# Reordering the first loads and the first chunk's copies in a fused attention and gated-MLP kernel

## The chip, the cores and the metric

The kernel runs on one core of one Trainium2 chip. The metric is the device time of one execution in microseconds (us), as a median of several. A core has a matrix engine (TensorE, "PE" in the profile, with its weight loads as "PEld"), VectorE ("DVE"), ScalarE ("ACT"), GpSimd ("POOL") and SyncE ("SP"). SP and ACT issue the DMAs of this kernel, each on a queue of its own. The times here differ by tenths of a microsecond in 266, so two things are kept apart throughout: the time of the unprofiled rounds, and the position of single instructions in one profiled execution.

## The reference, cut to what matters

One layer normalisation feeds an attention branch (32 heads of 16, a sliding window of 256) and a bilinear gated MLP; both are added to the input.

```python
def reference(x, wqkv, wo, w_gate, w_up, w_down):     # x 1x2048x512, F = 1792
    xn = layernorm(x)
    q, k, v = split(xn @ wqkv)                        # 32 heads of 16
    p = softmax(where(causal & within 256, q k^T / 4, -1e9))
    a = (p v) @ wo
    b = ((xn @ w_gate) * (xn @ w_up)) @ w_down
    return x + a + b
```

## The kernel before: the parts that matter

The 2048 tokens are worked in 4 chunks of 4 tiles of 128 tokens. Chunk 0 has to be made before any score can be computed. For each tile x is loaded, VectorE takes statistics, ScalarE the root, VectorE the reciprocal and the scaling, TensorE transposes, and then come the projections to values, keys and queries. The kernel has a list scheduler written in Python: it walks a model of the engines, with estimated landing times, and emits each instruction where the model starts it. So the order on each engine is fixed when the program is built, and the constants in the model decide it. Two of them are penalties in us: 0.3 makes ScalarE less attractive for an operation that VectorE can take too, and HOLD puts off operations that are not on the chain to the next transpose, until the first scores are placed. At the start and behind tile 0's transpose TensorE runs filler matmuls of ones.

```python
# loads, in order of issue (two queues)
load(nc.sync,   Wqkv[:, 0:2, 1024:1536], ...)   # half of Wv on SP
load(nc.scalar, x[:, 0, :], ...)                # x0 on ACT
load(nc.sync,   Wqkv[:, 2:4, 1024:1536], ...)   # other half of Wv on SP
load(nc.scalar, x[:, 1, :], ...)                # x1 on ACT
for t, lo in ((2, 512), (3, 0)):                # Wk, x2, Wq, x3 on SP
    load(nc.sync, Wqkv[:, :, lo:lo + 512], ...)
    load(nc.sync, x[:, t, :], ...)
... # Wg, Wu, rest of x, Wd in four pieces, Wo
# which engine takes an operation: the least of
key = (at + (0.3 if e == "A" and len(o.on) > 1 else 0.0) + (HOLD if o.rank and now0 else 0.0), o.rank, t)
...
# chunk 0 as the model sees it (us)
land = (3.4, 3.95, 7.7, 9.6)      # x0 to x3
wv, wk, wq = 5.9, 7.3, 9.3
# tile 1's statistics are taken in two halves; the first may run before tile 0 is scaled
...
def project(i, lo, tok=tok):      # keys or queries of one tile, into one PSUM bank
    for c in range(4):
        matmuls(M[i][:, 128*c:128*c+128], [(Wqkv[:, k, lo+128*c:...], xnT[0][:, k, tok]) for k in range(4)])
```

The softmax here doesn't subtract the row's maximum and nothing guards it: scores larger than these inputs give would overflow.

Of the kernel before, what the change touches and what calls it, by code (L numbers as in the profile page):

```python
# [18 lines left out]
SWITCH = 0.11  # L19
PE_LAT = {"V": 0.22, "A": 0.31}  # L20
LAT = 0.06
PSUM_COPY = {"V": (0.605, 0.69), "A": (0.49, 0.60)}


# [61 lines left out]
class Kernel:  # L86
# [2 lines left out]
    PACE = 2.9  # L89
    SHARE = 1.0  # L90
    FEED = 0.1
    HOLD = 0.1

    def __init__(self, live=True):
        self.live = live
# [47 lines left out]
    def prologue(self):  # L143
        nc = self.nc
        xv = self.x_d.rearrange("(t p) d -> p t d", p=128)
        w = {k: v.rearrange("(k p) n -> p k n", p=128) for k, v in self.w_d.items()}

        def load(eng, dst, src):
            eng.dma_start(out=dst, in_=src)  # L149

        load(nc.sync, self.Wqkv[:, 0:2, 1024:1536], w["qkv"][:, 0:2, 1024:1536])
        load(nc.scalar, self.x[:, 0, :], xv[:, 0, :])
        load(nc.sync, self.Wqkv[:, 2:4, 1024:1536], w["qkv"][:, 2:4, 1024:1536])
        load(nc.scalar, self.x[:, 1, :], xv[:, 1, :])
        for t, lo in ((2, 512), (3, 0)):
            load(nc.sync, self.Wqkv[:, :, lo:lo + 512], w["qkv"][:, :, lo:lo + 512])
            load(nc.sync, self.x[:, t, :], xv[:, t, :])
        h = self.F // 2
        for lo in (0, h):
            load(nc.sync, self.Wg[:, :, lo:lo + h], w["g"][:, :, lo:lo + h])  # L160
            load(nc.sync, self.Wu[:, :, lo:lo + h], w["u"][:, :, lo:lo + h])
            if lo == 0:
                load(nc.sync, self.x[:, 4:8, :], xv[:, 4:8, :])
        load(nc.sync, self.x[:, 8:NT, :], xv[:, 8:NT, :])
        for f, g in ((0, 4), (4, 8), (8, 11), (11, 14)):
            load(nc.sync, self.Wd[:, f:g], w["d"][:, f:g])
        load(nc.sync, self.Wo[:], w["o"])
        for _ in range(4):
            nc.sync.drain()

        c = self.const
        nc.gpsimd.memset(self.ident[:], 0.0)
        nc.gpsimd.affine_select(out=self.ident[:], in_=self.ident[:], compare_op=ALU.not_equal, fill=1.0,
                                base=0, pattern=[[-1, 128]], channel_multiplier=1)
        nc.gpsimd.memset(self.mhalf[:], -0.5)
        warm = c.tile([128, 1], F32, name="warm")
        nc.vector.memset(warm[:], 0.0)
        nc.vector.memset(self.eps[:], 1e-5)
        nc.scalar.activation(out=warm[:], in_=warm[:], func=ACT.Sqrt)
        self.warm = warm  # L180
        pi = c.tile([128, 1], I32, name="pi")
        nc.gpsimd.iota(pi[:], pattern=[[0, 1]], base=0, channel_multiplier=1)
        podd = c.tile([128, 1], I32, name="podd")
        nc.vector.tensor_scalar(out=podd[:], in0=pi[:], scalar1=4, scalar2=1,
                                op0=ALU.arith_shift_right, op1=ALU.bitwise_and)
        nc.vector.tensor_copy(out=self.own[:, 1:2], in_=podd[:])
        nc.vector.tensor_scalar(out=self.own[:, 0:1], in0=podd[:], scalar1=0, scalar2=None, op0=ALU.is_equal)
        nc.gpsimd.memset(self.V[0][:, :, :, 16:18], 1.0)
        self.keep_busy(42, 0)
# [98 lines left out]
    def run(self):  # L288
        if self.live:
            self.prologue()  # L290
        self.now, self.mode = 5.4, "D"
        self.free = {"V": 3.0, "A": 4.5, "G": 3.0, "S": 6.0}
        self.waiting, self.log, self.idle = [], [], []
        self.banks = [0.0] * 4
        self.s_free, self.p_free = 0.0, [0.0] * self.PBUFS
        self.at_ = {}
        self.A, self.B = [], []
        self.g = self.v = 0
        self.first_s = None
        self.credit = 0.0  # L300
        self.pairs = [(T, c) for T in range(NCH) for c in range(4)]
        self.batches, self.of_pair = [], []
        for T, c in self.pairs:
            batches = layout(T)
            self.of_pair.append(range(len(self.batches), len(self.batches) + len(batches)))
            self.batches += [(T, c, b) for b in batches]
        self.list_work()
        self.loop()
        return max(self.now, *self.free.values(), *(o for o in self.at_.values() if isinstance(o, float)))
# [20 lines left out]
    def loop(self):  # L330
        while True:
            best, now0 = None, self.first_s is None
            for o in self.waiting:
                t = self.when(o.deps)
                if t is None:
                    continue
                for e, (took, lat) in o.on.items():
                    at = max(t, self.free[e])
                    key = (at + (0.3 if e == "A" and len(o.on) > 1 else 0.0) + (self.HOLD if o.rank and now0 else 0.0), o.rank, t)
                    if best is None or key < best[0]:  # L340
                        best = (key, o, e, at)
            p = self.choose()
            if p is not None and (best is None or p[0] <= best[3]):
                self.do(*p)
                continue
            if best is None:
                break
            _, o, e, at = best
            took, lat = o.on[e]
            o.start, o.eng, o.end = at, e, at + lat + LAT  # L350
            self.free[e] = at + took
            self.waiting.remove(o)
            self.log.append((at, e, took, o.name))
            if self.live:
                o.emit(e)
            for f in o.then:
                f(o)
        left = [o.name for o in self.waiting] + [d.name for d in self.A] + [d.name for d in self.B]
        assert not left and self.g == len(self.batches) and self.v == len(self.pairs), left[:9]
# [215 lines left out]

    def first_chunk(self):

        land = (3.4, 3.95, 7.7, 9.6)
        wv, wk, wq = 5.9, 7.3, 9.3
        nc = self.nc  # L580
        roots = []
        for b in range(4):
# [26 lines left out]
                self.at_["ap", b, n] = self.op(f"ap{b}", {"V": took}, [s], lambda e, b=b, cols=cols: self.i_apply(b, cols), rank=0)  # L609
        self.op("table", {"A": (1.5, 1.5)}, roots + [("Q", 0, 0, 2)], lambda e: nc.scalar.activation(  # L610
            out=self.warm[:], in_=self.warm[:], func=ACT.Exp), rank=1)
        last = self.op("masks", {"V": (0.15, 0.2)}, [self.at_["ap", 1, 0]], lambda e: nc.vector.memset(self.masks[:], -1), rank=9)
        for n in range(5):
            last = self.op("masks", {"G": (0.4, 0.5)}, [last], lambda e, n=n: self.i_masks(n), rank=9)
        self.at_["masks",] = last
# [3 lines left out]
        for b in range(4):  # L619
            tok = slice(128 * b, 128 * b + 128)  # L620
# [13 lines left out]
                x.then.append(lambda o: self.at_.update({("begun", 0, b, ks.start): o.start}))  # L634

            def project(i, lo, tok=tok):
                for c in range(4):
                    self.matmuls(self.M[i][:, 128 * c:128 * c + 128],
                                 [(self.Wqkv[:, k, lo + 128 * c:lo + 128 * c + 128], self.xnT[0][:, k, tok]) for k in range(4)])

            def k_out(o, i, b=b):
                x = o
                for lane in range(2):
                    x = self.op(f"K0b{b}", PSUM_COPY, [o, x], lambda e, lane=lane: self.i_keys(
                        e, 0, slice(0, 4), lane, self.M[i].rearrange("p (c t) -> p c t", c=4), slice(2 * b, 2 * b + 2)), rank=1)
                self.frees(x, i)
                for c in range(4):
                    self.at_["K", 0, c, b] = x
# [53 lines left out]
    def add_qk(self, T, c):  # L702
        def emit(i, lo):
            self.matmuls(self.M[i][:], [(self.Wqkv[:, k, lo:lo + 128], self.xnT[T % 2][:, k, :]) for k in range(4)])

        def k_out(o, i):
            x = o
            for lane in range(2):
                x = self.op(f"K{T}.{c}", PSUM_COPY, [o, x], lambda e, lane=lane: self.i_keys(
                    e, T, slice(c, c + 1), lane, self.M[i].unsqueeze(1)), rank=1)  # L710
            self.frees(x, i)
            for b in range(4):
                self.at_["K", T, c, b] = x

        def q_out(o, i):
            x = self.op(f"Q{T}.{c}", PSUM_COPY, [o], lambda e: self.copy(e, self.Q[T % 2][:, c, :], self.M[i][:]), rank=1)
            self.frees(x, i)
            for b in range(4):
                self.at_["Q", T, c, b] = x

        old = self.ring(T, 2) if T == 3 else []
        self.add(f"k{T}.{c}", 4, self.xT(T) + old, lambda i: emit(i, 512 + 128 * c), k_out)
        self.add(f"q{T}.{c}", 4, self.xT(T) + self.ring(T, 2), lambda i: emit(i, 128 * c), q_out)
# [109 lines left out]
```

## Time and profile before

| | before |
|---|---|
| time, median of the first 3 runs | 265.79 us (265.54 to 265.85) |
| profiled span | 264.0 us |
| TensorE busy | 259.4 us (98%) |
| first transpose, third transpose, first scores on TensorE | 5.53, 10.58, 17.33 us |
| start of TensorE's last matmul, and from it to the end of the span | 260.22, 3.76 us |

TensorE is the bound: from the first transpose on it holds work with no pause over 0.3 us. Read such a profile by asking where its queue has holes, and then which chain feeds the work that stands behind the hole. The lines are in the prediction.

### The profile page before, as it was taken

How to read it: one execution, taken by the hardware profiler on the slowest of the kernel's cores; microseconds unless marked ns; L12 is line 12 of the kernel's file. 1: busy time of each engine (PE TensorE's matmuls, PEld its weight loads, DVE VectorE, ACT ScalarE, POOL GpSimd, SP SyncE). 2: the span in 40 equal slices, each digit the busy share in tenths (PEclk: the TensorE clock that was granted, in tenths of full speed). 3: DMA queues.
4: the chain of work that ended last, by engine and by line, in shares of the span. 5: the costliest groups of instructions: out<-in, count | busy, mean ns of one | idle time of the engine just before them, and what ended most of it. 6: DMA issues, size and time to landing. Idle time of an engine off the chain costs nothing.

```text
span 264.0 us, 8009 instructions
## 1 busy us (share of the span) xinstructions
PE 259.4 (98%) x3456; PEld 131.9 (50%) x3456; DVE 190.6 (72%) x368; ACT 165.0 (63%) x122; POOL 119.7 (45%) x272
## 2 busy tenths in 40 slices
PE   8999999999999999999999999999999999999994
PEld 7974444554444354455534354546535353545462
DVE  4999886978996548777997467786946268786504
ACT  3457576768776766687776767677777676572000
POOL 1406655475175635427084736437081828255000
PEclk9999999999999999999999999999999999999999
DMA  6999910000002200000005200000000100000002
GB/s 219 381 374 350 215 22 1 2 0 2 4 2 59 64 22 22 0 2 2 2 0 83 62 22 0 4 2 0 2 2 22 40 4 22 2 0 2 0 2 81
DMA packets 17251, 13.88 MB, mean 53 GB/s; under 512 B 7104, under 2 KB 17216, under 8 KB 17216
## 3 DMA queue, kind: packets, MB, share of 16 engines
q1 hardware_dynamic: 16784, 13.05, 18.0%
q8 instruction: 27, 0.44, 0.7%
q10 hardware_dynamic: 432, 0.33, 0.4%
q14 instruction: 8, 0.07, 0.1%
HBM read 9.70 MB, written 2.10 MB: 45 GB/s over the span
## 4 chain that ended last, share of the span: by engine, by line
PE 96%; DMA 2%; DVE 1%; ACTq 0%; issue 0%
PE M L207 72%; PE S L215 9%; PE M L245 7%; PE M L689 6%; DMA x<-in_A_x_dram 1%; DMA out_dram<-xn 1%; PE M L624 1%; PE S L207 1%; DVE xn L783 1%; DVE st L591 0%; ACTq L149 0%; DVE xn L273 0%; PE M L197 0%; DVE rs L603 0%
## 5 line engine op out<-in xcount | busy, mean ns | idle before, releaser
L498 ACT ACTIVATE P<-S 128x2048 bf16<-128x2048 f32 x76 | 140.9, 1854 | 57.1 <-PE S L215 50.5
L224 POOL TENSOR_SCALAR_AFFINE_SELECT P<-P 64x256 bf16<-64x256 bf16 (+1 forms) x248 | 112.6, 456 | 112.9 <-ACT P L498 100.7
L207 PE MATMUL M<-xnT,Wg 128*128 128x512 bf16 x224 | 57.7, 380 | 0.0
L207 PE MATMUL M<-xnT,Wu 128*128 128x512 bf16 x224 | 57.7, 380 | 0.0
L207 PE MATMUL M<-Wd,hT 128*128 128x512 bf16 (+1 forms) x224 | 51.8, 373 | 0.0
L741 DVE TENSOR_TENSOR hT<-M,gsb 128x512 bf16<-128x512 f32 x56 | 38.0, 678 | 8.4 <-PE M L207 8.1
L207 PEld LDWEIGHTS <-hT 128*128 128x128 bf16 x238 | 21.7, 98 | 23.4 <-issue 2.1
L207 PEld LDWEIGHTS <-Wu 128*128 128x128 bf16 x224 | 20.5, 98 | 24.8 <-issue 1.8
L207 PEld LDWEIGHTS <-Wg 128*128 128x128 bf16 x224 | 20.2, 98 | 24.3 <-issue 2.4
L203 DVE CAST gsb<-M 128x512 bf16<-128x512 f32 x41 | 28.1, 686 | 5.3 <-PE M L207 4.9
L207 PE MATMUL M<-xnT,Wqkv 128*128 128x128 bf16 (+1 forms) x224 | 30.3, 288 | 0.0
L215 PE MATMUL S<-Q,K 32*128 32x320 bf16 (+3 forms) x720 | 30.0, 254 | 0.0
L534 DVE STREAM_TRANSPOSE at<-M 128x512 f32<-128x512 f32 x32 | 21.3, 698 | 9.7 <-PE M L245 9.6
L215 PEld LDWEIGHTS <-K 32*128 32x128 bf16 x720 | 11.9, 92 | 31.8 <-issue 30.9
L230 DVE TENSOR_TENSOR P<-P,masks 128x512 int16<-128x512 int16 x56 | 22.6, 410 | 7.1 <-ACT P L498 7.1
L207 PEld LDWEIGHTS <-Wqkv 128*128 128x128 bf16 x224 | 15.9, 98 | 10.6 <-issue 1.5
L783 DVE TENSOR_TENSOR y<-M,x 128x512 bf16<-128x512 f32 x12 | 8.2, 687 | 16.5 <-PE M L207 16.3
L245 PE MATMUL M<-P,V 64*17 64x320 bf16 (+4 forms) x1440 | 19.5, 252 | 0.0
L245 PEld LDWEIGHTS <-V 64*17 64x17 bf16 x1440 | 17.1, 86 | 3.2 <-issue 1.3
L284 DVE TENSOR_SCALAR K<-M,own 128x512 bf16<-128x512 f32 x24 | 17.1, 743 | 2.1 <-PE M L207 2.1
L207 PE MATMUL M<-Wo,OT 128*128 128x512 bf16 (+1 forms) x64 | 16.6, 374 | 0.0
L689 PE MATMUL M<-Wqkv,xnT 128*64 128x256 bf16 x256 | 15.5, 274 | 0.0
(51 smaller groups left out, 138.0 us busy)
## 6 DMA issues: line engine op xcount, KB each, us to landing
Wg<-in_B_w_gate_dram SPq DMA_DIRECT2D x2, 896.0 KB, 10.2
Wu<-in_B_w_up_dram SPq DMA_DIRECT2D x2, 896.0 KB, 11.9
out_dram<-y SPq DMA_DIRECT2D x12, 128.0 KB, 1.7
Wqkv<-in_A_wqkv_dram SPq DMA_DIRECT2D x2, 512.0 KB, 6.1
x<-in_A_x_dram SPq DMA_DIRECT2D x1, 1024.0 KB, 13.6
Wd<-in_B_w_down_dram SPq DMA_DIRECT2D x2, 512.0 KB, 11.6
Wd<-in_B_w_down_dram SPq DMA_DIRECT2D x2, 384.0 KB, 8.7
Wqkv<-in_A_wqkv_dram SPq DMA_DIRECT2D x2, 256.0 KB, 3.5
```

Source lines behind the costliest of these rows:

```text
L203: self.nc.vector.tensor_copy(out=out, in_=in_)
L207: self.nc.tensor.matmul(ps, lhsT=a, rhs=b, start=first and n == 0, stop=last and n == len(pairs) - 1)
L215: self.nc.tensor.matmul(self.S[:, e, 64 * at:64 * (at + m)], lhsT=self.K[U % 3][rows, c, j].rearrange("p l t -> p (l t)"), rhs=self.Q[T % ...
L224: self.nc.gpsimd.affine_select(out=v, in_=v, pattern=[[0, 4], [0, n], [sign, 64]], base=0, fill=0.0, compare_op=ALU.is_gt if kind else ALU ...
L230: self.nc.vector.tensor_tensor(out=v, in0=v, in1=m, op=ALU.bitwise_and)
L245: self.nc.tensor.matmul(banks[lane][32 * e:32 * e + 17, 64 * q:64 * (q + m)], lhsT=self.V[U % 3][rows, j, 4 * c + e, 0:17], rhs=P[rows, e, ...
L284: self.nc.vector.tensor_scalar(out=out, in0=in_, scalar1=own, scalar2=None, op0=ALU.mult)
L498: ex = self.op(f"exp{g}", {"A": (took + 0.06, took + 0.18)}, [o], lambda e: self.nc.scalar.activation(out=P[:, :, 0:hi], in_=self.S[:, :, ...
L534: t = self.op(f"tr{v}", {"V": (0.63, 0.71)}, [o] + ts, lambda e, par=par: nc.vector.transpose(out=self.at[:, :, par, :], in_=self.M[banks[ ...
L689: self.nc.tensor.matmul(self.M[i][64 * lane:64 * lane + 64, 256 * jj:256 * jj + 256], lhsT=self.xnT[T % 2][:, k, tok], rhs=w[:, lane], sta ...
L741: x = self.op(f"u{T}.{f}", {"V": PSUM_COPY["V"]}, [o, ("gate", T, f)], lambda e: self.nc.vector.tensor_tensor(out=self.hT[T % 2][:, f, :], ...
L783: self.nc.vector.tensor_tensor(out=keep["y"][:, cols], in0=self.M[i][:, cols], in1=self.x[:, t, cols], op=ALU.add)
```

## The change

The intent is to have tile 1 and the second half of Wv arrive in balance on two queues, to let key projections begin when half of their weights are there, and to spread chunk 0's copies evenly over VectorE and ScalarE. The core of the diff (Wd in three pieces in place of four, new estimates for the key copies, earlier start times of the model for TensorE and ScalarE, and the mask memset after tile 3 in place of tile 1 are left out):

```diff
-        load(nc.sync, self.Wqkv[:, 2:4, 1024:1536], ...)
-        load(nc.scalar, self.x[:, 1, :], xv[:, 1, :])
-        for t, lo in ((2, 512), (3, 0)): ...
+        load(nc.sync, self.x[:, 1, :], xv[:, 1, :])
+        load(nc.scalar, self.Wqkv[:, 2:4, 1024:1536], ...)
+        load(nc.sync, self.Wqkv[:, 0:2, 512:1024], ...)      # key weights, two k halves
+        load(nc.sync, self.Wqkv[:, 2:4, 512:1024], ...)
 ...
-    HOLD = 0.1
+    HOLD = 0.2
-  key = (at + (0.3 if e == "A" and len(o.on) > 1 else 0.0) + ...
+  key = (at + (0.3 if e == "A" and len(o.on) > 1 and not now0 else 0.0) + ...
-        land = (3.4, 3.95, 7.7, 9.6);   wv, wk, wq = 5.9, 7.3, 9.3
+        land = (3.4, 4.0, 8.0, 9.85);   wv, wk, wq = 5.2, 7.1, 9.5
-                for c in range(4):
-                    self.matmuls(self.M[i][:, 128 * c:...], [... for k in range(4)])
+                for k in range(4):
+                    for c in range(4):
+                        self.nc.tensor.matmul(self.M[i][:, 128 * c:...], ..., start=k + c == 0, stop=k == 3)
```

More of the change, by code (lines that the diff above doesn't have):

```diff
@@ L21 @@
 LAT = 0.06
+KEYS_COPY = {"V": (0.68, 0.76), "A": (0.63, 0.70)}
 PSUM_COPY = {"V": (0.605, 0.69), "A": (0.49, 0.60)}
@@ L152, in prologue @@
         load(nc.scalar, self.x[:, 0, :], xv[:, 0, :])
-        load(nc.sync, self.Wqkv[:, 2:4, 1024:1536], w["qkv"][:, 2:4, 1024:1536])
-        load(nc.scalar, self.x[:, 1, :], xv[:, 1, :])
-        for t, lo in ((2, 512), (3, 0)):
-            load(nc.sync, self.Wqkv[:, :, lo:lo + 512], w["qkv"][:, :, lo:lo + 512])
-            load(nc.sync, self.x[:, t, :], xv[:, t, :])
+        load(nc.sync, self.x[:, 1, :], xv[:, 1, :])
+        load(nc.scalar, self.Wqkv[:, 2:4, 1024:1536], w["qkv"][:, 2:4, 1024:1536])
+        load(nc.sync, self.Wqkv[:, 0:2, 512:1024], w["qkv"][:, 0:2, 512:1024])
+        load(nc.sync, self.Wqkv[:, 2:4, 512:1024], w["qkv"][:, 2:4, 512:1024])
+        load(nc.sync, self.x[:, 2, :], xv[:, 2, :])
+        load(nc.sync, self.Wqkv[:, :, 0:512], w["qkv"][:, :, 0:512])
+        load(nc.sync, self.x[:, 3, :], xv[:, 3, :])
         h = self.F // 2
@@ L164, in prologue @@
         load(nc.sync, self.x[:, 8:NT, :], xv[:, 8:NT, :])
-        for f, g in ((0, 4), (4, 8), (8, 11), (11, 14)):
+        for f, g in ((0, 5), (5, 10), (10, 14)):
             load(nc.sync, self.Wd[:, f:g], w["d"][:, f:g])
@@ L290, in run @@
             self.prologue()
-        self.now, self.mode = 5.4, "D"
-        self.free = {"V": 3.0, "A": 4.5, "G": 3.0, "S": 6.0}
+        self.now, self.mode = 4.8, "D"
+        self.free = {"V": 3.0, "A": 3.4, "G": 3.0, "S": 6.0}
         self.waiting, self.log, self.idle = [], [], []
@@ L338, in loop @@
                     at = max(t, self.free[e])
-                    key = (at + (0.3 if e == "A" and len(o.on) > 1 else 0.0) + (self.HOLD if o.rank and now0 else 0.0), o.rank, t)
+                    key = (at + (0.3 if e == "A" and len(o.on) > 1 and not now0 else 0.0) + (self.HOLD if o.rank and now0 else 0.0), o.rank, t)
                     if best is None or key < best[0]:
@@ L576, in first_chunk @@
     def first_chunk(self):
-        land = (3.4, 3.95, 7.7, 9.6)
-        wv, wk, wq = 5.9, 7.3, 9.3
+        land = (3.4, 4.0, 8.0, 9.85)
+        wv, wk, wq = 5.2, 7.1, 9.5
         nc = self.nc
@@ L611, in first_chunk @@
             out=self.warm[:], in_=self.warm[:], func=ACT.Exp), rank=1)
-        last = self.op("masks", {"V": (0.15, 0.2)}, [self.at_["ap", 1, 0]], lambda e: nc.vector.memset(self.masks[:], -1), rank=9)
+        last = self.op("masks", {"V": (0.15, 0.2)}, [self.at_["ap", 3, 0]], lambda e: nc.vector.memset(self.masks[:], -1), rank=9)
         for n in range(5):
@@ L636, in project @@
             def project(i, lo, tok=tok):
-                for c in range(4):
-                    self.matmuls(self.M[i][:, 128 * c:128 * c + 128],
-                                 [(self.Wqkv[:, k, lo + 128 * c:lo + 128 * c + 128], self.xnT[0][:, k, tok]) for k in range(4)])
+                for k in range(4):
+                    for c in range(4):
+                        self.nc.tensor.matmul(
+                            self.M[i][:, 128 * c:128 * c + 128], lhsT=self.Wqkv[:, k, lo + 128 * c:lo + 128 * c + 128],
+                            rhs=self.xnT[0][:, k, tok], start=k + c == 0, stop=k == 3, skip_group_check=True)
             def k_out(o, i, b=b):
@@ L643, in k_out @@
                 for lane in range(2):
-                    x = self.op(f"K0b{b}", PSUM_COPY, [o, x], lambda e, lane=lane: self.i_keys(
+                    x = self.op(f"K0b{b}", KEYS_COPY, [o, x], lambda e, lane=lane: self.i_keys(
                         e, 0, slice(0, 4), lane, self.M[i].rearrange("p (c t) -> p c t", c=4), slice(2 * b, 2 * b + 2)), rank=1)
@@ L708, in k_out @@
             for lane in range(2):
-                x = self.op(f"K{T}.{c}", PSUM_COPY, [o, x], lambda e, lane=lane: self.i_keys(
+                x = self.op(f"K{T}.{c}", KEYS_COPY, [o, x], lambda e, lane=lane: self.i_keys(
                     e, T, slice(c, c + 1), lane, self.M[i].unsqueeze(1)), rank=1)
```

## The prediction

> **What bounds the kernel now.** I read the page first, for the busy shares. Then the view of who waited for whom, TensorE alone; then the timeline from 0 to 18 us, where every changed instruction but the later key copies lies; then the landing times of the first DMAs.
>
> The page:
>
> ```profile
> PE 259.4 (98%) x3456; PEld 131.9 (50%) x3456; DVE 190.6 (72%) x368; ACT 165.0 (63%) x122; POOL 119.7 (45%) x272
> PE 96%; DMA 2%; DVE 1%; ACTq 0%; issue 0%
> ```
>
> TensorE is busy 259.4 of 264.0 us, and the chain that ends last runs over it for 96%. Busy is not yet working, so I asked for its waits; this is the whole answer:
>
> ```profile
> PE M L197 <- PEq L817: 0.8, 1, 0.8
> PE M L624 <- DVE xn L273: 0.2, 1, 0.2
> ```
>
> Two waits in 264 us: 0.8 us of start-up and 0.2 us before the first transpose (line 624). The last copies and stores after TensorE's end make up the rest, and the change leaves them alone. So the kernel is one TensorE queue from 5.53 us on, and time can be won only where that queue holds less than it shows. I therefore compared the start-to-start distances of single matmuls, which the views merge, with the distance in the middle of a run: 56 ns for a 128-column matmul, 216 ns for a 512-column one, 109 ns for a lane pair of value projections. From 17.3 us to the end nothing exceeds these but the step from one kind of block to another (312 in place of 216 ns at the end of a dense block, about 0.1 us each). All real slack is before 10.6 us:
>
> ```profile
> 5.53 0.54 PE L624 MATMUL M<-ident,xn 128*128 128x128 bf16 x4 [0.22 <-DVE xn L273]
> 5.91 0.39 PE L197 MATMUL M<-const-bfloat16-1.0 128*128 128x128 bf16 x4
> 6.29 1.06 PE L689 MATMUL M<-Wqkv,xnT 128*64 128x256 bf16 x16
> 7.40 0.40 PE L624 MATMUL M<-ident,xn 128*128 128x128 bf16 x4
> 7.63 2.92 PE L207 MATMUL M<-xnT,Wqkv 128*128 128x128 bf16 x48
> 10.58 0.40 PE L624 MATMUL M<-ident,xn 128*128 128x128 bf16 x4
> 10.81 1.95 PE L207 MATMUL M<-xnT,Wqkv 128*128 128x128 bf16 x32
> ```
>
> The columns are start, duration, instruction, count. The reader is to see: the 48 projections need 48 x 0.056 = 2.68 us, but 2.95 us pass until the next transpose. In the single starts, 0.08 us is lost after the first 16 and 0.19 us at the end, waiting for tile 2's transpose. The same count gives 0.21 us before tile 1's transpose at 7.40, and 0.15 + 0.38 us around the split first transpose, fillers included. With the 0.22 us wait that is 0.22 + 0.53 + 0.21 + 0.08 + 0.19 = 1.23 us of slack, **0.5% of the time**: all that a change to the prologue can reach. From 10.58 to 17.3 us the queue has no holes.
>
> Why the first transpose is late (VectorE, ScalarE):
>
> ```profile
> 4.14 0.18 DVE L593 BATCH_NORM_AGGREGATE mv<-st 128x2 f32<-128x6 f32 x1
> 4.35 0.29 ACT L600 ACTIVATE ve<-mv,eps 128x1 f32<-128x1 f32 x1 [1.12 <-DVE mv L593]
> 4.60 0.43 DVE L591 BATCH_NORM_STATS2 st<-x 128x6 f32<-128x256 bf16 x1 [0.29 <-DMA x<-in_A_x_dram]
> 4.95 0.15 DVE L603 RECIPROCAL rs<-ve 128x1 f32<-128x1 f32 x1
> ```
>
> The root was ready at 4.64 us, but its reciprocal stands behind tile 1's first half of statistics, which waited until 4.58 us for x1 to land. That holds the chain by 4.95 - 4.70 = about 0.25 us.
>
> **What the Trainium skill says.** "TensorE: Matmul & The Clock Gate", Architectural detail, says ScalarE and VectorE are strict FIFO: the trace agrees (the reciprocal at 4.95 with its input ready at 4.64). The same page, Back-to-back issue gap, gives N/2.4 + 2.5 ns, so 56 ns at 128 columns, but about 81 ns for sustained pairs of load and matmul; this trace has 56 ns with a fresh weight load each, so no pair cost is there for the new loop order to save. "DMA: Bandwidth & Descriptors", Issuing engines are not separate DMA queues, says queues of SP and ACT share the same 16 engines and interleave: the packets of both queues do overlap here from 2.4 to 4.3 us. "PSUM — Partial Sum Buffer", The four PSUM rules, says a first-matmul flag clears a whole bank's bits, so one flag per bank serves k by k; no run shows that yet.
>
> **The change part by part.**
>
> *Loads.* The same bytes are moved; only order and queue differ. x1 landed at 1.25 + 3.33 = 4.58 us; by the packets, ACT's queue finished x0 near 3.0 and x1 near 4.2, SP's the first half of Wv at 3.6 and the second at 4.57 us. Starved stretches (SP's queue moves only 6 to 12 KB per 0.1 us at 3.6 to 3.8 us, against 37 later) look like issues served one after another: x0, Wv, x1, Wv. Now x1 is second on SP, so its packets begin near 3.6 us and share the engines with the 256 KB on ACT: 128 KB at half of 37 KB per 0.1 us is 0.7 us, done at 4.3; landings came 0.4 us after, so 4.7 us, or 5.0 if it goes strictly last. My choice is 4.75: **+0.15 us** at the first transpose. At best x1 lands before 4.3, and the gain stops at 0.25, as the fillers end near 5.3 us. Wv needed by 6.29 landed at 5.1; either way it is in time. Key weights landed near 7.5, and key projections start at 7.63: not a wait now, but it would be one if everything moved 0.2 us earlier. The two halves remove that, worth nothing by themselves. Bytes ahead of x2, Wq and x3 are the same, so about 7.9, 9.35 and 9.7 us stay; the new constants in the source suggest 0.2 later.
>
> *k by k.* 128 matmuls at 56 ns either way: **0**.
>
> *Copies alike.* In the loop, ScalarE loses a penalty of 0.3 in chunk 0. By walking the rule by hand I get the same TensorE order (first transpose, values 0, transpose 1, keys 0 and 1, queries 0, transpose 2), but tile 1's transposed copy goes to ScalarE, where it takes 0.60 in place of 0.41 us on VectorE but starts near 7.87, not 8.14. So keys 1 need not wait: **-0.08 us**. VectorE loses that copy, and the mask memset (0.33 us, at 7.35) moves behind tile 3. Its value copy then starts near 7.42, not 7.59, and tile 2's statistics near 8.1 in place of 8.46. The walk still puts one key copy (0.72 us) ahead of tile 2's reciprocal, so its normalised tile comes near 10.3, not 10.52: **-0.19 us** at most. Queries 0 would start at 9.42 and may wait for Wq at about 9.4 to 9.55: +0.05 to 0.1 of it back.
>
> *Later.* Key copies of later chunks are only estimated longer; no instruction changes, and nothing there waits. But the greedy order will shift, and each block more or less costs about 0.1 us: 0 +- 0.2. Three Wd loads for four: hidden, 0.
>
> Sum: +0.15 - 0.08 - 0.19 + 0.07 = **-0.05 us**, spread about 0.35.
>
> **Rivals.** (a) x1 lands earlier than now. For: someone put it ahead of the second half of Wv on SP and set the model's start to 4.8. Against: the sharing above. It would add -0.25 and give near 265.2. (b) x1 goes strictly last and lands at 5.0: first transpose +0.4, half of it absorbed, about 266.0. (c) VectorE or ScalarE becomes the bound before the first scores: VectorE is busy 6.57 of 6.70 us from 10.6 to 17.3, ScalarE 4.05. For a loss: a root behind a 0.63 us key copy on ScalarE delays a transpose. For a gain: ScalarE takes work. TensorE has gate and up blocks to fill in, so either is worth little. (d) The larger hope, scores starting earlier and everything with them: not supported, as the score pace only places blocks in a full queue, and 16 us of dense work (243.9 to 260.2 us) follows the last attention block.
>
> **Range and chances.** The sum says 265.7; as (a) is what the edit aims at and an edit of a tuned kernel is rarely made to lose, I lean to **265.55 us**. The slack of 1.23 us caps a gain near 264.6; a loss over 0.7 needs two bad terms. Eight in ten: 264.9 to 266.2. 2% is 5.3 us, over four times the slack: within 2% 0.98, each side 0.01.
>
> **What would show it.** x1's landing (4.58 now), the reciprocal (4.95), the first transpose (5.53), the third (10.58), the end of the last query projection (15.50): I expect about 4.75, 5.1, 5.7, 10.5, 15.4. TensorE's waits stay at two, and the prologue's difference plus 0.1 us per block more or fewer should be the whole difference. Wrong if TensorE shows a new wait after 17.3 us, if the 128 projections leave 56 ns, or if a block order with several more switches costs over 0.5 us.

## The result, and the profile after

The changed kernel took **266.41 us** (median of 6 runs, 266.16 to 266.46) against 265.75 us for the kernel before. The ratio is 1.0021 (95% interval 1.0008 to 1.0034): the mean time of one kernel's fast runs over that of the other's of the same rounds, so not quite the ratio of the medians. That is about 0.6 us slower, clear of noise, far within 2%, and outside the range stated. All runs count as fast: none was more than 1.5% above the fastest of its kernel.

The page of the changed kernel has less busy time on TensorE in a longer span, so the difference is waiting:

```profile
span 264.5 us, 7999 instructions
PE 259.0 (98%) x3456; PEld 131.4 (50%) x3456; DVE 189.0 (71%) x364; ACT 167.0 (63%) x126; POOL 119.7 (45%) x272
```

TensorE's waits are again two, but the 0.2 us before the first transpose (line 624 before, 627 now) has become 1.4 us (columns: us in total, times, longest):

```profile
PE M L627 <- DVE xn L276: 1.4, 1, 1.4
PE M L200 <- PEq L822: 0.8, 1, 0.8
```

The timeline of TensorE in the changed kernel (start, duration, instruction, count; fillers and the lines from 13.64 to 18.14 left out), to be laid beside the one in the prediction:

```profile
6.32 0.54 PE L627 MATMUL M<-ident,xn 128*128 128x128 bf16 x4 [1.39 <-DVE xn L276]
7.08 1.06 PE L694 MATMUL M<-Wqkv,xnT 128*64 128x256 bf16 x16
8.18 0.40 PE L627 MATMUL M<-ident,xn 128*128 128x128 bf16 x4
8.42 2.84 PE L642 MATMUL M<-xnT,Wqkv 128*128 128x128 bf16 x48
11.10 0.39 PE L627 MATMUL M<-ident,xn 128*128 128x128 bf16 x4
11.32 1.06 PE L642 MATMUL M<-xnT,Wqkv 128*128 128x128 bf16 x16
12.53 1.05 PE L642 MATMUL M<-xnT,Wqkv 128*128 128x128 bf16 x16
13.42 0.39 PE L627 MATMUL M<-ident,xn 128*128 128x128 bf16 x4
18.14 0.40 PE L218 MATMUL S<-Q,K 32*128 32x256 bf16 x8
```

The first transpose is at 6.32 in place of 5.53 us. (That is 0.79 us, while the wait grew by 1.17: the fillers before it ended 0.39 us earlier in this execution.) The 48 projections from 8.42 now need 2.68 us until the next transpose, where they needed 2.95. After queries 1 (from 11.32) there is a new hole: the next 16 projections (keys 2) start at 12.53, where 16 x 0.056 after 11.32 would be 12.22.

VectorE in the changed kernel shows why the first transpose is late:

```profile
4.23 0.18 DVE L596 BATCH_NORM_AGGREGATE mv<-st 128x2 f32<-128x6 f32 x1
5.39 0.43 DVE L594 BATCH_NORM_STATS2 st<-x 128x6 f32<-128x256 bf16 x1 [0.97 <-DMA x<-in_A_x_dram]
5.73 0.15 DVE L606 RECIPROCAL rs<-ve 128x1 f32<-128x1 f32 x1
```

The order is the one of before: tile 1's first half of statistics stands ahead of tile 0's reciprocal. But it waited for x1 until 5.37 us, where it waited until 4.58 before. Here is the account of the two profiled spans, each step read from where TensorE stands (from starts rounded to 0.01 us):

| from | before | after | difference |
|---|---|---|---|
| to the first transpose | 5.53 | 6.32 | +0.79 |
| to the third transpose | 5.05 | 4.78 | -0.27 |
| to the fourth transpose | 2.02 | 2.32 | +0.30 |
| to the first scores | 4.73 | 4.72 | -0.01 |
| to TensorE's last matmul | 242.89 | 243.00 | +0.11 |
| to the end of the span | 3.76 | 3.34 | -0.42 |
| sum | 263.98 | 264.48 | +0.50 |

Two theories could explain this. Theory 1: x1's later landing is the cause; it reaches TensorE by the order on VectorE, and the new copies give and take about the same (0.27 us before the third transpose, 0.30 after it). Theory 2: the new sharing of copies and the block order cost the time, and the late tile would have been absorbed by the holes behind it.

### The profile page after: what moved, and what is told of

It reads as the page before. It is cut to its first block, busy times and chain, and to the rows that moved or that the text cites. A ratio compares the mean times of both kernels' runs of the same rounds, so it can differ in the third digit from the quotient of the medians.

```text
span 264.5 us, 7999 instructions
## 1 busy us (share of the span) xinstructions
PE 259.0 (98%) x3456; PEld 131.4 (50%) x3456; DVE 189.0 (71%) x364; ACT 167.0 (63%) x126; POOL 119.7 (45%) x272
## 4 chain that ended last, share of the span: by engine, by line
PE 94%; DMA 2%; DVE 2%; ACT 0%; issue 0%; SPq 0%
PE M L210 69%; PE S L218 9%; PE M L248 7%; PE M L694 6%; DMA x<-in_A_x_dram 2%; PE M L642 1%; DVE st L594 1%; DMA out_dram<-xn 1%; PE S L210 1%; DVE xn L788 1%; DVE xn L276 0%; PE M L627 0%; DVE V L206 0%; DVE K L287 0%; ACT xnT L204 0%
## 5 line engine op out<-in xcount | busy, mean ns | idle before, releaser
L206 DVE CAST gsb<-M 128x512 bf16<-128x512 f32 x40 | 27.4, 686 | 6.4 <-PE M L210 6.1
L210 PE MATMUL M<-xnT,Wqkv 128*128 128x512 bf16 x96 | 23.0, 380 | 0.0
L287 DVE TENSOR_SCALAR K<-M,own 128x512 bf16<-128x512 f32 x22 | 15.7, 742 | 2.6 <-PE M L210 1.9
L204 ACT ACTIVATE gsb<-M 128x512 bf16<-128x512 f32 x16 | 9.6, 599 | 8.0 <-PE M L210 7.9
```

Of the source, the lines that this page charges most:

```text
L206: self.nc.vector.tensor_copy(out=out, in_=in_)
L210: self.nc.tensor.matmul(ps, lhsT=a, rhs=b, start=first and n == 0, stop=last and n == len(pairs) - 1)
L287: self.nc.vector.tensor_scalar(out=out, in0=in_, scalar1=own, scalar2=None, op0=ALU.mult)
```

## The experiments

All kernels but the two repeats differ from one of the two by a few lines, all gave correct results, and each was timed in 5 rounds beside the kernel before on the same chip (its median there was 265.54 to 265.71 us).

**The change with the old queues.** Only the queues of x1 and the second half of Wv go back.

```diff
 # on the changed kernel
-        load(nc.sync, x[:, 1, :]);  load(nc.scalar, Wqkv[:, 2:4, 1024:1536])
+        load(nc.sync, Wqkv[:, 2:4, 1024:1536]);  load(nc.scalar, x[:, 1, :])
```

> The changed kernel with one thing undone: x1 behind x0 on ACT and both halves of Wv on SP again. Theory 1 (x1's landing is the cause): x1 lands near 4.6 us in place of 5.37, the first transpose starts near 5.5 us in place of 6.32, and the time falls by 0.6 to 0.9 us to about 265.6, a little under or at the kernel before. Theory 2 (the new sharing of copies between ScalarE and VectorE and the block order cost the time, and the late tile is absorbed): stays above 266.1.

Measured: 265.38 us (265.31 to 266.02), ratio to before 0.9993 (0.9981 to 1.0005). x1 landed at 4.31 us, and these are the first transpose and the first scores:

```profile
5.27 0.64 PE L627 MATMUL M<-ident,xn 128*128 128x128 bf16 x4
17.24 0.40 PE L218 MATMUL S<-Q,K 32*128 32x256 bf16 x8
```

Undoing this one exchange takes back the whole loss.

**The exchange alone.** The same two lines exchanged in the kernel before, nothing else.

```diff
 # on the kernel before
-        load(nc.sync, Wqkv[:, 2:4, 1024:1536]);  load(nc.scalar, x[:, 1, :])
+        load(nc.sync, x[:, 1, :]);  load(nc.scalar, Wqkv[:, 2:4, 1024:1536])
```

> The kernel before with the one exchange: x1 on SP behind half of Wv, the other half on ACT behind x0. Theory 1: x1 lands near 5.3, the first transpose near 6.3, and the time rises by 0.7 to 0.8 us to about 266.5. Theory 2: the later holes close up (tile 2's transpose waited 0.19 us, tile 1's 0.21) and the time stays under 266.0.

Measured: 266.39 us, ratio 1.0032 (1.0020 to 1.0044). x1 landed at 5.37 us, as in the changed kernel, and the first scores came 0.79 us later than in the kernel before, as the first transpose did. Its wait for a tile, its VectorE timeline and its first scores:

```profile
PE M L624 <- DVE xn L273: 0.8, 1, 0.8
5.39 0.43 DVE L591 BATCH_NORM_STATS2 st<-x 128x6 f32<-128x256 bf16 x1 [1.05 <-DMA x<-in_A_x_dram]
5.74 0.15 DVE L603 RECIPROCAL rs<-ve 128x1 f32<-128x1 f32 x1
18.11 0.40 PE L215 MATMUL S<-Q,K 32*128 32x256 bf16 x8
```

Theory 1 stands, theory 2 falls: the holes behind did not close up at all (5.04 us from the first to the third transpose, 5.05 before). The landing view of the same stretch, for the kernel before and for this one (KB, us from issue to landing), puts it in two lines: the same 128 KB took 3.3 us on ACT behind x0, and 4.0 us on SP behind half of Wv. In all profiles taken, x1 landed at 5.28 to 5.37 us in the three with the new queues, and at 4.28 to 4.76 in eleven of the twelve with the old ones (the twelfth comes below).

```profile
x<-in_A_x_dram ACTq DMA_DIRECT2D x1, 128.0 KB, 3.3
```
```profile
x<-in_A_x_dram SPq DMA_DIRECT2D x1, 128.0 KB, 4.0
```

**Both tiles first.** Is SP slow, or is it what stands ahead of x1?

```diff
 # on the changed kernel: x1 stays on SP, but first
-        SP: half of Wv, x1, ...     ACT: x0, half of Wv
+        SP: x1, half of Wv, ...     ACT: x0, half of Wv
```

> The changed kernel with x1 still on SP and half of Wv still on ACT, but x1 ahead of SP's half of Wv. If x1 was late for what stood before it in SP's queue and shared the engines with it (my theory), x1 lands by 4.4 us and the time is near 265.4, like the old queues. If x1 was late because SP's queue as such is slow to start, it lands after 4.8 and the time stays above 266.

Measured: 265.51 us. x1 landed at 3.50 us, on SP. So it is not the queue, but what stands ahead of x1 and what shares the engines with it (256 KB and the other half of Wv in the change); the run does not part these two. But x0 landed at 3.67 us, later than the 3.3 to 3.5 of most other profiles, and the first transpose came at 5.57, no earlier than in the kernel before.

**The true landing told to the scheduler.** The loads of the change untouched; the estimate for x1 goes from 4.0 to 5.4 us, and with it tile 1's statistics go behind tile 0's reciprocal and scaling (later copies and projections shift as well).

```diff
 # on the changed kernel
-        land = (3.4, 4.0, 8.0, 9.85)
+        land = (3.4, 5.4, 8.0, 9.85)
```

> The changed kernel, loads untouched, with the scheduler told when x1 really lands (5.4 in place of 4.0), so that tile 0's reciprocal and scaling stand ahead of tile 1's statistics on VectorE. If x1 reached TensorE only through the queue order on VectorE, the first transpose is back near 5.4 us although x1 still lands near 5.4, and the time is near 265.7. If the late x1 costs whatever the order (tile 1 itself is needed), the first scores still start near 18.1 and the time stays near 266.3.

Measured: 265.70 us, with x1 landing at 5.28. Its VectorE and TensorE:

```profile
4.41 0.18 DVE L596 BATCH_NORM_AGGREGATE mv<-st 128x2 f32<-128x6 f32 x1
4.95 0.16 DVE L606 RECIPROCAL rs<-ve 128x1 f32<-128x1 f32 x1 [0.36 <-ACT ve L603]
5.15 0.60 DVE L276 TENSOR_SCALAR xn<-x,mv,rs 128x256 bf16<-128x256 bf16 x2
```
```profile
5.55 0.54 PE L627 MATMUL M<-ident,xn 128*128 128x128 bf16 x4 [0.86 <-DVE xn L276]
9.12 1.05 PE L642 MATMUL M<-xnT,Wqkv 128*128 128x128 bf16 x16 [0.52 <-DVE xnT L206]
17.64 0.40 PE L218 MATMUL S<-Q,K 32*128 32x256 bf16 x8
```

The reciprocal no longer waits for a tile that it does not need, and the first transpose is back at 5.55 us although x1 is as late as in the changed kernel. So the late landing did its harm through the order on VectorE. Of the first scores' delay 0.40 us remains (17.64 against 17.24 with the old queues). 0.28 of it is there at the first transpose: x0 landed at 3.65 us in this execution, at 3.30 in the other. The late tile itself now shows as a wait of 0.52 us before keys 1 (at 9.12), but the new order has no hole before keys 2, so that from the first transpose to the first scores it is 12.08 against 11.97 us.

**The new copies alone.** The kernel before with the changed scheduling, but its own loads and loop order.

```diff
 # on the kernel before: ScalarE's penalty off in chunk 0, HOLD 0.2, new landing and copy estimates,
 # start times of the model, mask memset after tile 3; nothing else
```

> The kernel before with the changed scheduling alone (ScalarE without its penalty in chunk 0, the new constants, the mask memset after tile 3), loads and loop order as before. Theory 1: the first transpose stays near 5.5, the third comes at 10.3 in place of 10.58, a hole of about 0.3 us before keys 2 gives it back, and the time is within 0.2 us of 265.75. Theory 2: 266.2 or more.

Measured: 265.80 us, ratio 1.0006 (0.9993 to 1.0019). The third transpose came at 10.34 us, though mostly because x1 landed at 4.28 us here and the first transpose came at 5.27. From the second to the third transpose it took 2.91 us in place of 3.18, as in the changed kernel, and the hole before keys 2 was 0.43 us. The copies give and take, as theory 1 has it. The end of this run is that of the changed kernel too: 3.30 us behind TensorE's last matmul, in place of 3.76.

**The loop and the key halves.**

```diff
 # on the kernel before: for k, for c in place of for c, for k; and the key weights in two loads
```

> The kernel before with key weights in two halves and chunk 0's projections k by k, nothing else. Theory 1: 56 ns a matmul as before, no difference over 0.15 us. Rival: interleaved sums in one bank cost time, then the 128 projections take more than 56 ns each and the time rises by more than 0.3 us.

Measured: 266.36 us, ratio 1.0029 (1.0017 to 1.0041). Neither expectation held: 0.6 us slower, with 56 ns a matmul as before. The next two runs split it.

> Half of the previous run that came out 0.6 us slower against every expectation: the kernel before with the k by k loop alone. Theory A (the loop order costs): near 266.3. Theory B (the key weights' two loads cost): near 265.7. Theory C (neither; a build has an offset of its own in when its first load lands and its last store is taken): near 265.7 too, but then the other half is no slower either.

The loop alone: 265.63 us, ratio 1.0005 (0.9992 to 1.0017). Nothing, as predicted.

> The other half: the kernel before with the key weights loaded in two k halves, old loop. Theory A: near 265.7. Theory B: near 266.3, with x1 or x0 landing later or the last store later than in the kernel before. Theory C: near 265.7.

The key halves alone: 266.44 us, ratio 1.0032 (1.0018 to 1.0045). Its first scores came at 17.36 us and TensorE's last matmul at 260.26, as in the kernel before. The loss is all behind that: 4.44 us to the end in place of 3.76. Here is the end in the kernel before and in this one (the SP line merges the last two stores, start and duration of both together):

```profile
260.38 0.81 SPq L790 DMA_DIRECT2D out_dram<-xn  x2
261.06 0.35 ACTq L790 DMA_DIRECT2D out_dram<-xn  x1
```
```profile
260.41 1.17 SPq L792 DMA_DIRECT2D out_dram<-xn  x2
261.09 0.35 ACTq L792 DMA_DIRECT2D out_dram<-xn  x1
```

SP issued the last of its stores 0.43 us later (at 261.25 against 260.82 us), though VectorE's result was there as before, and that store landed 2.14 us after its issue where it took 1.60. ACT's last store was issued as before, and it too landed late, 2.11 us after its issue in place of 1.63. The change itself does not show this. It has one load more for the keys and one less for Wd. The next two runs take that up.

```diff
 # on the kernel with the key halves; then, second, on the kernel before
-        for f, g in ((0, 4), (4, 8), (8, 11), (11, 14)):      # Wd in four loads
+        for f, g in ((0, 5), (5, 10), (10, 14)):              # in three
```

> The kernel before with the key weights in two loads and Wd in three in place of four, so SP issues as many DMAs as before. The key halves alone cost 0.7 us, all of it after TensorE's end (last store issued 0.43 us later, the end's waits 0.4 us longer). If that comes from one more DMA in SP's stream, this run is back at 265.65 and its last store follows within 0.5 us of TensorE's last matmul; if it comes from the key weights' smaller loads themselves, it stays near 266.4.

Measured: 265.57 us (265.36 to 265.63), and the end is as in the kernel before, 3.73 us behind TensorE's last matmul:

```profile
260.14 0.81 SPq L792 DMA_DIRECT2D out_dram<-xn  x2
260.82 0.35 ACTq L792 DMA_DIRECT2D out_dram<-xn  x1
```

So one DMA more on SP cost 0.7 us at the far end of the kernel. The change has as many as before, as it loads Wd in three pieces; the changed kernel with four was not run.

> The kernel before with Wd in three loads in place of four: one DMA less on SP. If only one more than before hurts (SP's stream then reaches a point it does not reach with fewer), this is 265.65 or a little less. If any change of the count hurts (the eight completion flags turn by one), it is near 266.3.

One DMA less: inconclusive, with a median of 266.03 us and a ratio of 1.0016 (1.0001 to 1.0031). Three of the six runs were at 265.64 to 265.85 us, three at 266.21 to 266.81, all at the full clock. The profile, of a run of 265.64, shows the ordinary end of 3.76 us. What the slower three had is not seen. What SP does in the gap of 0.43 us with one DMA more is open too. This profile shows something else: its first key projections waited 0.27 us (until 7.82) for the key weights, one load that landed at 7.78 us. That is the wait that the two halves are to remove; in the changed kernel the second half was there at 6.68.

**Tile 2's copy.** The hole before keys 2 stood behind ScalarE in the changed kernel:

```profile
10.36 1.27 ACT L285 ACTIVATE K<-M,own 128x512 bf16<-128x512 f32 x2 [0.34 <-DVE K L287]
11.70 0.29 ACT L603 ACTIVATE ve<-mv,eps 128x1 f32<-128x1 f32 x1
11.90 0.58 ACT L204 ACTIVATE xnT<-M 128x512 bf16<-128x512 bf16 x1
```

The transpose of tile 2 was on TensorE at 11.10 us, but its copy ran on ScalarE behind two key copies and tile 3's root. In the kernel before it ran on VectorE, and there was no hole:

```profile
11.26 0.39 DVE L203 COPY xnT<-M 128x512 bf16<-128x512 bf16 x1
```

The first try exchanges that copy with queries 0's copy:

```diff
 # on the changed kernel with the old queues
-        took = {"A": (0.48, 0.6), "V": (0.31, 0.41)} if len(ks) == 4 else ...
+        took = {"V": (0.31, 0.41)} if b == 2 else ...          # and HOLD 0.3
```

> The changed kernel with the old queues of x1 and Wv, and with tile 2's transposed copy and queries 0's copy exchanged between ScalarE and VectorE (nothing else in the two engines' order moves in chunk 0). If sharing the copies alike is what makes the 0.31 us hole before keys 2, the hole goes, and the time falls by 0.3 us against the run with the old queues alone, to about 265.1. If the hole comes from elsewhere (bank, weights), it stays and so does the time, 265.4.

Measured: 265.87 us, a miss for both sides. The scheduler answered by putting transpose 3 ahead of keys 2, where it waited 0.48 us for tile 3. Its profiled run also had x1 landing at 5.36 us with the old queues, and took 266.61 us; the other four took 265.62 to 266.02. So once in twelve profiles the old queues landed x1 as late as the new ones, and that run lost as much. The second try holds TensorE's order with one more dependence (transpose 3 after keys 2):

> The old queues in the changed kernel, tile 2's transposed copy on VectorE, and now TensorE's order held (transpose 3 after keys 2), which the earlier attempt did not hold. If the 0.31 us hole before keys 2 is tile 2's copy standing behind two key copies on ScalarE, keys 2 follow queries 1 without a hole and the first scores come 0.2 to 0.3 us earlier than with the old queues alone (17.24), with a time near 265.1. If the hole only moves to transpose 3, the time is 265.4 or more.

Measured: 265.52 us. The hole was gone, but the first scores came at 17.25 us as with the hole, because this execution began later: x1 landed at 4.54 us, the first transpose came at 5.49 in place of 5.27, and the second 2.12 us after it in place of 2.00 (the record of TensorE's full clock begins at 6.8 us here, at 5.9 there). So the pair was run again on one chip:

> The changed kernel with the old queues once more, unchanged, as the partner of the next run on the same chip: 265.4, with the hole of 0.3 us before keys 2.

> The closed hole once more, unchanged, on the same chip as the old queues. If the hole is a real part of the time: 0.3 us under its partner, 265.1. If start-up and the later waits absorb it: equal within 0.15 us.

Measured: 265.44 us with the hole, 265.29 without. The trace without it:

```profile
10.27 0.39 PE L627 MATMUL M<-ident,xn 128*128 128x128 bf16 x4
10.49 1.95 PE L642 MATMUL M<-xnT,Wqkv 128*128 128x128 bf16 x32
12.28 0.39 PE L627 MATMUL M<-ident,xn 128*128 128x128 bf16 x4
```

The 32 projections run through (10.49 to 12.28 us is 32 x 0.056), where the partner lost 0.31 us in the middle. From the third transpose to the first scores it is 6.74 against 7.05 us. In the time the medians differ by 0.15 us; one run of 267.20 us widens the interval (0.9977 to 1.0021 against before), and without it the means differ by 0.25. That is what the hole is worth by the trace, but these rounds alone do not prove it.

**A version ahead of both.** Both tiles first, and the closed hole.

> The closed hole of the previous run with x0 first on ACT and x1 first on SP, the halves of Wv behind them. If both gains add and x0 does not land later for it: 265.2, and ahead of the kernel before by 0.4. If x0 lands later beside x1 (3.67 in place of 3.3 to 3.5 in the run with both first), what is won behind is lost in front: 265.5.

Measured: **265.17 us** (264.98 to 265.36), ratio to before 0.9985 (0.9973 to 0.9997). The gain of 0.4 us is small, but its interval lies below 1. x0 landed at 3.65 us and the first transpose came at 5.55, so the front was not better than before. In the profile 0.15 us of the gain lie between there and the scores (11.65 in place of 11.79 us) and 0.47 at the end (3.28 in place of 3.76). So the exchange of the first loads does not earn it: beside the closed hole with the old queues (265.29, or 265.23 as a mean without the run of 267.20 us) it is the same within noise.

The ends of all profiled runs fall into three groups. With the old schedule it is 3.71 to 3.76 us from TensorE's last matmul to the end of the span, with one DMA more on SP 4.44 and 4.59, and with the new schedule 3.25 to 3.35. In the old schedule VectorE's last drain starts about 0.4 us after SP's and ACT's (263.47 against 263.08 us in the kernel before); in the new one it starts right beside them (264.06 against 264.03 in the changed one). VectorE has 364 instructions there in place of 368 (363 in one). That the new schedule makes the shorter end is shown by the run with the new copies alone. By what means is open. The traces have one hint: the transfers of 8 KB on the DMA queue that the profile lists as "q14 instruction", counted from 12 us before the span to just after it, are 17 in the two runs with one DMA more on SP, 16 in the five others of the old schedule, and 15 in the ten of the new one; the difference lies outside the span, one more before it or one fewer after it. With one DMA more the last of them inside the span (261.90 to 262.51 us in the key halves' run) runs while the last stores are moving; in the kernel before it begins at 262.27, when they are nearly done. That the length of the instruction streams moves the end fits this, and no run tests it.

## Why the prediction was wrong

- **The bound and the cap were right.** Between the first scores and TensorE's last matmul the two differ by 0.11 us (242.89 and 243.00). The difference was made before the scores and after the last matmul, as tenths of a microsecond.
- **The step that failed is x1's landing: "My choice is 4.75: +0.15 us at the first transpose".** It landed at 5.37 us and cost 0.79. The idea behind it (second on SP, sharing the engines with the half on ACT) held, and both terms were sized too small. The prediction had x1's last packet done at 4.3: by the packets in the trace it was done at 4.68, because from 3.6 to 3.9 us SP's queue moved at most 9 KB per 0.1 us while ACT's moved 27 to 35, and only then did they share about evenly, at 16 to 21 KB each. The prediction had seen such a starved stretch in the kernel before and left it out of this sum. And the landing was seen 0.69 us after the last packet, not 0.4. Rival (b), "lands at 5.0", came nearest of the four, still too mild. Its "half of it absorbed" failed too: the exchange alone passed its whole 0.79 us on to the first scores (17.33 to 18.11). What the changed kernel won back is the copies' doing.
- **What the reciprocal stands behind was right.** The same order carried the late tile to the first transpose, and the run with the true landing shows it by taking it away.
- **"-0.08" and "-0.19" held to the hundredth.** The third transpose regained 0.27 us, from 3.18 to 2.91 us after the second. The wait for Wq (+0.07) did not come: Wq landed at 9.16 us, before its first use at 10.2; with the old queues, too, it was there first (8.83 against 9.29).
- **A term was missing: the hole before keys 2, +0.30 us.** The prediction followed the copies by hand as far as the third transpose and took the rest for full, "From 10.58 to 17.3 us the queue has no holes". That was a fact about the order of before. ScalarE, freed of its penalty, took tile 2's copy too, behind two key copies. Rival (c) named the risk for a root, not for a copy. The run that puts the copy back on VectorE and holds TensorE's order shows the hole gone.
- **k by k, 0: right**, by its own run. "PSUM — Partial Sum Buffer", The four PSUM rules, held here: one first-matmul flag per bank served four interleaved sums, and every run with that loop gave correct results. **The two key halves "worth nothing by themselves"** was wrong in an unexpected place: alone they cost 0.7 us at the end of the kernel, and with the three Wd loads ("hidden, 0") beside them this cost was gone.
- **The end, "the change leaves them alone", was wrong** in the change's favour: 0.42 us less after the last matmul. Nobody had forecast it, so it is luck that the miss is not about 1 us. And none of the three signs named as "wrong if" came (no new wait after 17.3 us, 56 ns a projection, no cost of block switches over 0.5 us): they watched the middle of the kernel.
- **The lean was wrong.** The sum said 265.7 and I went lower because an edit is rarely made to lose. Summing again with the measured terms: 0.79 - 0.27 + 0.30 - 0.01 + 0.11 - 0.42 = +0.50 us in the profiled span, and about 0.56 in the time by the ratio.

## What to carry to other kernels

On an in-order engine, an instruction that waits for a transfer must not stand ahead of the head of the critical chain unless its data is surely there. Tell the scheduler the landing times that the trace shows: here that one constant took back the loss (265.70 us with 5.4, beside 265.66 for the kernel before; 266.41 with 4.0, beside 265.75). Do not put a small tile that the chain needs behind large weights on either queue; putting both tiles first of all brought x1 forward to 3.50 us, but with x0 at 3.67 beside it the first transpose was no earlier. In a kernel whose bound is one full queue, look at the few microseconds before it fills and after it empties; a change of load count in the front moved the end here by 0.7 us.

## What the Trainium skill lacked or had wrong

- "DMA: Bandwidth & Descriptors", Issuing engines are not separate DMA queues, says that issuing from several engines only saves the sequencer's time. The runs agree that the engines are shared. What the section does not say is how much the place in a queue, and what runs beside it, moves a landing: the same 128 KB took 2.7 us from its issue first on SP (0.80 to 3.50 us), 3.3 second on ACT behind 128 KB, and 4.0 second on SP behind 256 KB.
- The same page, Anatomy of one DMA — SWDGE (gpsimd) path, gives a fixed cost of about 2 us, about constant, for DMAs issued from GpSimd. I found no figure for the time from last packet to landing of DMAs issued from SP and ACT, as these are. It was 0.3 us (x1 before, 4.26 to 4.58) and 0.7 us (x1 after, 4.68 to 5.37).
- "TensorE: Matmul & The Clock Gate", Back-to-back issue gap, gives about 81 ns for sustained pairs of weight load and 128-column matmul. These traces have 56 ns over 48 pairs in a row in either loop order, and over 64 in the new one.
- No page that I found says that the time from TensorE's last matmul to the end depends on the count of loads or on the schedule: one DMA more on SP lengthened it from 3.76 to 4.44 us, and the new schedule, with four instructions fewer on VectorE, shortened it to 3.34.
